# Attention and soft mixture of experts on one core: a load asked for earlier and two small steps of the opening changed in order

## The chip, the cores and the metric

The kernel runs on one core of a Trainium2 chip. The metric is the device time of one execution in microseconds (us), the median of several runs. The core has five engines that work side by side, each through its own queue of instructions in order: TensorE (PE: matrix products and transposes), VectorE (DVE), ScalarE (ACT), GpSimd (POOL), and SyncE (SP), which here issues every transfer (DMA). Engines wait for one another through semaphores. Tiles lie in SBUF; TensorE writes its results to PSUM, of which the kernel uses eight tiles of one bank each.

## The reference

There are 8 batches of 8 heads, with 576 tokens and 64 values a head. The attention has a decay: the logarithm of a gate `f` is summed along the tokens, and the difference of two such sums is added to the score. The result is the input of a soft mixture of 8 experts with 4 slots each.

```python
scores = scale * np.matmul(q, k.transpose(0, 1, 3, 2))
cum = np.cumsum(np.log(np.clip(f, 0.0001, 1.0)), axis=-1)
scores = np.where(causal, -1e9, scores + cum[:, :, :, None] - cum[:, :, None, :])
attn = softmax(scores); x = attn @ v          # heads side by side: 4608 x 512
logits = x @ phi                              # 4608 x 32
slot_input = softmax(logits, axis=0).T @ x    # 32 slots
slot_out = relu(slot_input @ w1) @ w2         # by expert, 4 slots each
out = softmax(logits, axis=1) @ slot_out
```

## The kernel before

**Units.** The 64 heads are worked through in 32 pairs. Pair `g` holds heads `2g` and `2g+1`. Its queries and keys arrive in one load of 128 x 2 x 576 float32 values (`load_qk`, line 165) into one of three buffers, `RAW[g % 3]`: queries in rows 0 to 63, keys in rows 64 to 127. Its values arrive with `load_v` (line 170) into one of two halves of `V`.

**Two passes of products for a head.** The operands are rounded to a short form (fp32r) on ScalarE: `round_k` into `WA`, `round_q` into `YA` (lines 174 to 182), three buffers each. Beside the rounded values, some rows of these tiles carry the summed gates (`load_cum`) and the negative maximum of each query row. What the rounding left off is made on GpSimd (`low_k`, `low_q`, lines 199 to 208) into halves of `WB` and `YB`, two buffers each. The other halves of `WB` and `YB` are copies of the rounded operands, made by the transfers `dup_k` and `dup_q` (lines 190 to 197).

- The first pass, `s1` (line 213), makes scores with queries down the partitions, in four PSUM banks out of a set of three that is used in turn (tag `s`). `tops` (line 228) runs over them on VectorE and leaves the maximum of each query row.
- The maxima are turned by a transpose on TensorE and copied back as a row of `YA`. For pair 0 this is `first_rows` (line 560), in two steps separated by `yield`: five transposes, then two copies on ScalarE. For later pairs it is `mturn` and `mrows` (lines 242 to 259), with a transfer.
- The second pass, `s2` (line 261), makes the scores again with keys down the partitions, in six segments, each a product of the rounded operands (line 274) and one of the rest (line 275), into a ring of three PSUM banks. `expo` (line 278) takes the exponential on ScalarE and frees the bank. `causal` (line 283) sets what lies above the diagonal to zero on GpSimd.
- `s3` (line 301) multiplies with the values, fifty products a head; `norm` (line 316) divides on VectorE; `px` and `xcopy` turn the result for the logits.

**Order.** All order is written out by hand: a call in the Python program appends instructions to the queues of the engines it names, and nothing is reordered later. `warm(n, a)` (line 486) appends `n` products whose result nobody reads, to fill TensorE.

**The opening** (lines 492 to 647) prepares pairs 0 and 1 and the first pass of pair 2. It runs ahead of the main loop, whose pass `g` (line 681) does the second pass, masks, `s3` and `norm` of pair `g` and the first pass of heads `2g+3` and `2g+4`. `first(i, n, busy)` (line 573) appends products `n` of head `i`, then `busy` fillers, then the maxima of these products. `both(i, n)` appends products of the second pass and the exponential. In the opening, the load of pair 3 into `RAW[0]` stands at line 621, behind the transfers of `mrows(1, 0, 1)`, `load_v(1)`, `phis` and `mk`. `RAW[0]` also holds pair 0, whose last readers are `low_k(1)` and `low_q(1)` (lines 553 and 554). The roundings of pair 3 (lines 646 and 647) stand last in the opening, so in ScalarE's queue they come ahead of every exponential of the main loop's first pass, `g = 1`.

The queue of SP around the change holds, in order: `load_qk(2)`, `load_v(0)`, `dup_k(1)`, `dup_q(1)`, `load_cum(2)`, `mrows(1, 0, 1)`, `load_v(1)`, `phis`, `mk`, `load_qk(3)`, `mrows(1, 1, 2)`, `dup_q(2)`, `dup_k(2)`, `load_cum(3)`.

Of the kernel before, what the change touches and what calls it, by code (L numbers as in the profile page):

```python
# [24 lines left out]
WARM = (11, 1)  # L25
# [45 lines left out]
def attn_softmoe(ctx: ExitStack, tc: tile.TileContext, qk, v, f, phi, w1, w2, cst, out):  # L71
# [6 lines left out]
    cs = const.tile([P, 258], F32, name="cs")  # L78
# [69 lines left out]
    def pair(g):  # L148
        return 0 <= g < NG
# [15 lines left out]
    def load_qk(g):  # L165
        if pair(g) and ("r", g) not in st:
            st["r", g] = RAW[g % 3]
            nc.sync.dma_start(RAW[g % 3], qk[g])
# [5 lines left out]
    def round_k(g, *hs):  # L174
        if pair(g):
            for h in hs or range(2):
                nc.scalar.copy(WA[g % 3][0:64, S * h : S * h + S], RAW[g % 3][64:128, h])  # L177

    def round_q(g, *hs):
        if pair(g):  # L180
            for h in hs or range(2):
                nc.scalar.copy(YA[g % 3][0:64, h, 64:640], RAW[g % 3][0:64, h])  # L182
# [7 lines left out]
    def dup_k(g, h0=0, h1=2):  # L190
        if pair(g):
            s = slice(S * h0, S * h1)
            nc.sync.dma_start(WB[g % 2][64:128, s].bitcast(F32), WA[g % 3][0:64, s].bitcast(F32))

    def dup_q(g, h0=0, h1=2):
        if pair(g):
            nc.sync.dma_start(YB[g % 2][0:64, h0:h1].bitcast(F32), YA[g % 3][0:64, h0:h1, 64:640].bitcast(F32))
# [15 lines left out]
    def s1(i, *which):  # L213

        if not head(i):
            return
        g, h = divmod(i, 2)
        ya, wa, m = YA[g % 3], WA[g % 3][:, S * h : S * h + S], TOP[g % 3]
        for n in which:
            bank, o, blk, j0, w = TOPS[n]  # L220
            if o == 0:
                st["top", i % 2, bank] = scratch(False, f"s{i}_{bank}")
            t = st["top", i % 2, bank]
            nc.tensor.matmul(  # L224
                t[:, o : o + w], ya[0:m, h, 128 * blk : 128 * blk + 128], wa[0:m, j0 : j0 + w], start=True, stop=True
            )

    def tops(i, *which):
        if not head(i):
            return  # L230
        g, h = divmod(i, 2)
        for n in which:
            bank, o, blk, j0, w = TOPS[n]
            t = st["top", i % 2, bank]
            m0 = max(448 - (128 * blk + 64) + j0, 0)
            top = MT[g % 3][:, NBLK * h + blk : NBLK * h + blk + 1] if g else m2[h][:, blk, 1:2]
            nc.vector.tensor_tensor_reduce(  # L237
                out=t[:, o : o + w], in0=t[:, o : o + w], in1=mask[:, m0 : m0 + w], scale=1.0, scalar=top if n == 3 else -3.0e38,
                op0=ALU.add, op1=ALU.max, accum_out=top,
            )  # L240
# [245 lines left out]
    def warm(n, a, w=192):  # L486

        for _ in range(n):
            nc.tensor.matmul(ring[0][:, 0:w], a[:, 0:128], a[:, 0:w], start=True, stop=True)
# [83 lines left out]
    def first(i, n, busy=0):  # L573
        s1(i, *GROUPS[n])
        warm(busy, cs)
        tops(i, *GROUPS[n])
# [5 lines left out]
    r0, r1 = first_rows(0), first_rows(1)  # L582
    for n in range(4):
        first(0, n, WARM[1])
    first(1, 0, 2 * WARM[1])
    next(r0)
    warm(3 * WARM[1], cs)
    next(r0)
    round_q(1, 0)
    first(1, 1)  # L590
    first(1, 2)
    both(0, 0)
    first(1, 3)
# [1 line left out]
    both(0, 2)  # L595
    round_k(1, 1)
    round_q(1, 1)
    dup_k(1)
    dup_q(1)
    load_cum(2)  # L600
# [17 lines left out]
    load_v(1)  # L618
    nc.sync.dma_start(phis, phi)
    nc.sync.dma_start(mk, cst[:, 706:714])  # L620
    load_qk(3)
    round_q(2)
    both(1, 2)
    first(3, 1)
# [439 lines left out]
```

## Time and profile before

| | |
|---|---|
| median of 3 runs | 405.67 us (404.69 to 407.14) |
| the profiled execution | 407.26 us |
| its span, first to last instruction | 405.5 us |
| TensorE products busy | 385.3 us (95%) |
| VectorE busy | 281.7 us (69%) |
| ScalarE busy | 259.2 us (64%) |
| GpSimd busy | 257.6 us (64%) |
| mean granted TensorE clock | 0.986 |

A row of the order of instructions gives the start in us from the begin of the span, the length in us, the engine, the line of the kernel, the operation, the tile written and the tiles read with their shapes, and how many instructions are merged in the row (x). In brackets stands how long the engine was idle ahead of it, and what it is inferred to have waited for. Where several semaphores were waited for, the one named is the last that the profile shows; where the engine named had long been done, the real one was another, often a transfer. A row of stretches gives start and end, the length, the busy time of each engine with its count of instructions, the granted clock of TensorE (1.00 is full speed), the busy share of the 16 DMA engines, and GB/s.

### The profile page before, as it was taken

Reading aid. Unit: us, or ns where it says so; the run is one execution under the profiler, and the core shown is the slowest. Engines: PE = TensorE matmul, PEld = TensorE weight load, DVE = VectorE, ACT = ScalarE, POOL = GpSimd, SP = SyncE. Lnnn points to the kernel's source line nnn. Section 1 sums busy time; section 2 is a strip of 40 time slices with the busy share of each in tenths; the row PEclk is TensorE's granted clock in tenths of the full one; section 3 lists DMA queues with packets and bytes.
Section 4 is the critical chain, followed back from the end, with each engine's and each line's share of the span. In section 5 each row is a group of like instructions: output and inputs, shape, how many; then the busy total and the mean of one; then the engine's idle time right before and its main releaser. Section 6 shows DMA issues by size and latency. Waiting matters only on the chain.

```text
span 405.5 us, 15191 instructions
## 1 busy us (share of the span) xinstructions
PE 385.3 (95%) x5871; PEld 339.3 (84%) x5871; DVE 281.7 (69%) x1127; ACT 259.2 (64%) x660; POOL 257.6 (64%) x351
## 2 busy tenths in 40 slices
PE   7888999999999999999999999999999999899990
PEld 6678999999999999998999999999999885345780
DVE  7784787878787977796879787878787533312571
ACT  8847776767786777686767786778685443100561
POOL 4694788777777777787778777877787742120000
PEclk9996999999999999999999999999999999999997
DMA  6773566677867787768767767777765699999698
GB/s 207 183 183 108 150 174 181 204 205 210 254 192 221 207 238 211 203 191 254 200 197 210 221 205 206 205 207 206 203 172 152 227 360 375 381 408 391 239 368 335
DMA packets 35192, 93.72 MB, mean 231 GB/s; under 512 B 4282, under 2 KB 10096, under 8 KB 35120
## 3 DMA queue, kind: packets, MB, share of 16 engines
q1 hardware_dynamic: 35120, 92.75, 74.0%
q8 instruction: 46, 0.75, 0.8%
q14 instruction: 26, 0.21, 0.1%
HBM read 63.93 MB, written 9.73 MB: 182 GB/s over the span
## 4 chain that ended last, share of the span: by engine, by line
PE 81%; DMA 4%; DVE 3%; ACT 3%; issue 1%; POOL 0%; SPq 0%; DVEq 0%; ACTq 0%
PE pv L309 24%; PE ring L274 13%; PE ring L275 11%; PE s L224 11%; PE pv L336 4%; DMA RAW<-in_qk 3%; PE lg L372 2%; PE pv L911 2%; PE ds L453 2%; PE ring L874 2%; PE pv L874 2%; PE more L992 2%; DVE s L237 1%; DMA out<-RAW 1%; PE ring L911 1%; PE ring L992 1%
## 5 line engine op out<-in xcount | busy, mean ns | idle before, releaser
L281 ACT ACTIVATE PTS<-ring 128x320 f32<-128x320 f32 (+2 forms) x256 | 119.7, 513 | 64.3 <-PE ring L275 36.7
L237 DVE CUSTOM_DVE_ANT_0 s<-s,mask 128x320 f32<-128x320 f32 (+4 forms) x320 | 137.7, 449 | 10.4 <-PE s L224 5.9
L274 PE MATMUL ring<-YA,WA 67*128 67x320 f32 (+9 forms) x384 | 123.3, 334 | 2.7 <-ACT PTS L281 1.7
L275 PE MATMUL ring<-YB,WB 128*128 128x320 f32 (+4 forms) x384 | 111.7, 299 | 0.0
L309 PE MATMUL pv<-V,PTS 128*64 128x65 f32 x3200 | 105.0, 224 | 0.6 <-ACT mr L256 0.6
L309 PEld LDWEIGHTS pv<-V,PTS 128*64 128x64 f32 x3200 | 100.3, 138 | 3.2 <-issue 1.2
L224 PE MATMUL s<-WA,YA 66*128 66x288 f32 (+9 forms) x384 | 98.9, 314 | 1.6 <-ACT YA L182 0.8
L203 POOL TENSOR_TENSOR WB<-RAW,WB 64x576 fp32r<-64x576 f32 x64 | 90.3, 1411 | 11.7 <-DMA WB<-WA 4.9
L208 POOL TENSOR_TENSOR YB<-RAW,YA 64x576 fp32r<-64x576 f32 x64 | 89.3, 1413 | 2.4
L274 PEld LDWEIGHTS ring<-YA,WA 67*128 67x128 f32 (+3 forms) x384 | 70.6, 185 | 9.0 <-issue 2.1
L275 PEld LDWEIGHTS ring<-YB,WB 128*128 128x128 f32 (+1 forms) x384 | 70.8, 184 | 0.0
L224 PEld LDWEIGHTS s<-WA,YA 66*128 66x128 f32 (+1 forms) x384 | 63.6, 192 | 7.3 <-ACT YA L182 1.1
L289 POOL TENSOR_SCALAR_AFFINE_SELECT PTS<-PTS 128x384 f32<-128x384 f32 x64 | 33.3, 521 | 32.0 <-ACT PTS L281 27.8
L292 POOL TENSOR_SCALAR_AFFINE_SELECT PTS<-PTS 128x128 f32<-128x128 f32 (+1 forms) x128 | 31.3, 265 | 34.8 <-ACT PTS L281 32.1
L237 DVE DVE_READ_ACCUMULATOR2_ANT MT<- 128x1 f32 x372 | 52.7, 142 | 0.0
L177 ACT CAST WA<-RAW 64x576 fp32r<-64x576 f32 x64 | 40.0, 669 | 14.2 <-DMA RAW<-in_qk 13.2
L336 PE MATMUL pv<-cs,X 128*128 128x128 f32 x155 | 42.9, 278 | 1.0 <-DVE X L329 0.8
L182 ACT CAST YA<-RAW 64x576 fp32r<-64x576 f32 x64 | 40.0, 670 | 0.4
L237 DVE CUSTOM_DVE_ANT_0 s<-s,mask,MT 128x288 f32<-128x288 f32 x62 | 32.6, 526 | 9.8 <-PE s L224 0.9
L324 DVE TENSOR_SCALAR rl<-pv 128x5 f32<-128x5 f32 x64 | 10.5, 164 | 34.7 <-PE pv L309 33.8
L329 DVE TENSOR_TENSOR X<-pv,rl 128x320 f32<-128x320 f32 (+1 forms) x65 | 31.5, 486 | 2.4 <-DMA YA<-mr 0.3
L360 ACT COPY XT<-pv 128x128 f32<-128x128 f32 (+1 forms) x124 | 28.7, 292 | 0.0
(202 smaller groups left out, 355.1 us busy)
## 6 DMA issues: line engine op xcount, KB each, us to landing
w<-in_w SPq DMA_DIRECT2D x46, 512.0 KB
RAW<-in_qk SPq DMA_DIRECT2D x31, 576.0 KB
V<-in_v SPq DMA_DIRECT2D x32, 325.0 KB
WB<-WA SPq DMA_DIRECT2D x31, 288.0 KB
YB<-YA SPq DMA_DIRECT2D x31, 288.0 KB
p<-in_w SPq DMA_DIRECT2D x7, 512.0 KB
out<-RAW SPq DMA_DIRECT2D x5, 512.0 KB
out<-RAW SPq DMA_DIRECT2D x9, 256.0 KB
```

Of the source, the lines that this page charges most:

```text
L177: nc.scalar.copy(WA[g % 3][0:64, S * h : S * h + S], RAW[g % 3][64:128, h])
L182: nc.scalar.copy(YA[g % 3][0:64, h, 64:640], RAW[g % 3][0:64, h])
L203: nc.gpsimd.tensor_tensor(t[0:64], RAW[g % 3][64:128, h], t[64:128].bitcast(F32), op=ALU.subtract)
L208: nc.gpsimd.tensor_tensor(YB[g % 2][64:128, h], RAW[g % 3][0:64, h], YA[g % 3][0:64, h, 64:640].bitcast(F32), op=ALU.subtract)
L224: nc.tensor.matmul(t[:, o : o + w], ya[0:m, h, 128 * blk : 128 * blk + 128], wa[0:m, j0 : j0 + w], start=True, stop=True)
L237: nc.vector.tensor_tensor_reduce(out=t[:, o : o + w], in0=t[:, o : o + w], in1=mask[:, m0 : m0 + w], scale=1.0, scalar=top if n == 3 else ...
L274: nc.tensor.matmul(o, wa[0:m, j0 : j0 + n], ya[0:m, h, 64 + i0 : 64 + i0 + w], start=True, stop=False)
L275: nc.tensor.matmul(o, wb[:, j0 : j0 + n], yb[:, h, i0 : i0 + w], start=False, stop=True)
L281: nc.scalar.activation(PT[i % 2][:, SEG_O[bank] : SEG_O[bank] + at], t[:, 0:at], AF.Exp, scale=0.125)
L289: nc.gpsimd.affine_select(d3, d3, pattern=[[0, 3], [1, 128]], compare_op=ALU.is_ge, fill=0.0, base=0, channel_multiplier=-1)
L309: nc.tensor.matmul(o[64 * u : 64 * u + 64, t, :], PT[i % 2][:, at : at + 64], V[:, g % 2, c, 65 * h : 65 * h + 65], start=(c == 0), stop=( ...
L336: nc.tensor.transpose(pm[:, 0:128], x[:, t, 128 * (p % 2) : 128 * (p % 2) + 128], ident)
```

## The change

Three things are changed, all in the opening. `load_qk(3)` moves up in SP's queue, from behind `mk` to ahead of `dup_k(1)`. The second product group of head 1, `first(1, 1)`, moves from behind `round_q(1, 0)` to ahead of head 0's transposes (the first `next(r0)`). And the fillers around it change in number: two behind the first group of head 1 become one behind each of the first two groups, and three behind the transposes become two, so one filler in all goes. No other instruction is added or taken away.

```diff
     for n in range(4):
         first(0, n, WARM[1])
-    first(1, 0, 2 * WARM[1])
+    first(1, 0, WARM[1])
+    first(1, 1, WARM[1])
     next(r0)
-    warm(3 * WARM[1], cs)
+    warm(2 * WARM[1], cs)
     next(r0)
     round_q(1, 0)
-    first(1, 1)
     first(1, 2)
     both(0, 0)
     first(1, 3)
...
     round_k(1, 1)
     round_q(1, 1)
+    load_qk(3)
     dup_k(1)
     dup_q(1)
     load_cum(2)
...
     load_v(1)
     nc.sync.dma_start(phis, phi)
     nc.sync.dma_start(mk, cst[:, 706:714])
-    load_qk(3)
     round_q(2)
```

## The prediction

> **What bounds the kernel now.** I read the page first, then the busy time of each engine in chosen stretches, then the order of instructions of one engine at a time around the places that the change touches. The page's line of the TensorE clock, in slices of 10.1 us, has one hole in its middle, the fourth slice:
>
> ```profile
> PEclk9996999999999999999999999999999999999997
> ```
>
> The stretches around it (length, then busy us and instructions of each engine, clock, DMA share, GB/s):
>
> ```profile
> 15.57:18.98 3.41, 2.36 (x19) 1.89 (x17) 3.08 (x15) 3.30 (x7) 1.15 (x5) 1.00 0.69 227
> 22.40:25.81 3.41, 3.15 (x73) 2.81 (x69) 2.48 (x13) 1.11 (x4) 3.23 (x5) 1.00 0.68 163
> 29.23:32.64 3.41, 1.74 (x13) 1.51 (x13) 1.64 (x8) 3.39 (x9) 0.91 (x2) 1.00 0.87 283
> 32.64:39.47 6.83, 6.83 (x52) 6.37 (x53) 4.06 (x16) 3.92 (x11) 3.44 (x8) 0.50 0.05 16
> 26.98:41.86 14.88, 12.43 (x145) 11.39 (x143) 8.69 (x35) 9.49 (x21) 8.92 (x12) 0.77 0.53 138
> 41.86:50.73 8.87, 8.87 (x144) 8.48 (x143) 7.25 (x30) 6.82 (x17) 6.90 (x11) 1.00 0.49 142
> ```
>
> The last row is the second pass of the main loop: TensorE is busy for all of its 8.87 us, so a pass is worth what TensorE takes. The first pass, 26.98 to 41.86, does the same work in 14.88 us, 6.01 us more. Of that 3.41 us are the clock: from 32.64 to 39.47 TensorE is busy without a gap at 0.50 (6.83 x 0.5). The rest are gaps:
>
> ```profile
> 23.98 0.38 PE L224 MATMUL s<-WA,YA 66*128 66x288 f32 x1
> 24.61 0.92 PE L309 MATMUL pv<-V,PTS 128*64 128x65 f32 x24 [0.26 <-ACT mr L256]
> ...
> 29.01 0.33 PE L336 MATMUL pv<-cs,X 128*128 128x128 f32 x1 [0.78 <-DVE X L329]
> ...
> 29.83 0.27 PE L336 MATMUL pv<-cs,X 128*128 128x128 f32 x1
> 31.78 0.39 PE L274 MATMUL ring<-YA,WA 67*128 67x256 f32 x1 [1.67 <-ACT PTS L281]
> ```
>
> 0.78 us before 29.01 wait for VectorE's normalisation, 1.67 us before 31.78 for an exponential of ScalarE, which has to free a bank of the ring. ScalarE's order tells why that exponential is late:
>
> ```profile
> 24.30 0.25 ACT L256 CAST mr<-pv 5x128 fp32r<-5x128 f32 x1 [1.05 <-PE pv L247]
> 28.78 1.24 ACT L177 CAST WA<-RAW 64x576 fp32r<-64x576 f32 x2 [4.22 <-DMA RAW<-in_qk]
> 30.04 1.25 ACT L182 CAST YA<-RAW 64x576 fp32r<-64x576 f32 x2
> 31.19 1.17 ACT L281 ACTIVATE PTS<-ring 128x448 f32<-128x448 f32 x3
> ```
>
> The roundings of the fourth pair (round_k(3), round_q(3)) stand ahead of the first pass's exponentials in ScalarE's queue and wait 4.22 us for that pair's load. SP issues the load at 23.56, so it took 5.22 us:
>
> ```profile
> 13.87 0.33 SPq L172 DMA_DIRECT2D V<-in_v  x1
> 17.09 0.48 SPq L193 DMA_DIRECT2D WB<-WA  x1
> ...
> 23.56 0.37 SPq L168 DMA_DIRECT2D RAW<-in_qk  x1
> ```
>
> So the chain is: late load, late roundings, late exponential, TensorE idle, and behind it the slow clock.
>
> **Part one, the load.** load_qk(3) moves in SP's queue from behind phis and mk to ahead of dup_k(1), the row at 17.09, which waits there for ScalarE's rounding. It writes RAW[0], whose last reader is low_q(1), the first row here:
>
> ```profile
> 13.86 1.42 POOL L208 TENSOR_TENSOR YB<-RAW,YA 64x576 fp32r<-64x576 f32 x1
> ...
> 20.38 1.41 POOL L203 TENSOR_TENSOR WB<-RAW,WB 64x576 fp32r<-64x576 f32 x1 [1.57 <-PE ring L275]
> ...
> 23.82 0.49 POOL L292 TENSOR_SCALAR_AFFINE_SELECT PTS<-PTS 128x128 f32<-128x128 f32 x2
> ```
>
> It ends at 15.28, so SP issues the load at about 15.3 in 0.37 us and is free long before 17.09: the issue itself costs nothing. Even at the 5.22 us of the old load it lands by 20.5, before ScalarE is free at 24.55 (24.30 + 0.25). The roundings then run from 24.57 to 27.1 (28.78 to 31.29 is 2.51 us), and the first exponential follows its own product, which stands ahead of the row at 29.01. An exponential takes 0.6 us with its signal (31.19 to 31.78), so the ring is free by 29.6, before TensorE asks at 30.10 (29.83 + 0.27). **The gap of 1.67 us goes: -1.67.**
>
> **The clock.** In the stretch before the drop TensorE was busy for 1.74 of 3.41 us; at 2.36 of 3.41 (15.57 to 18.98) the clock stayed at 1.00. Without the gap the first of these has 1.74 + 1.67 = 3.41 busy. The 0.78 stays, but alone it leaves 2.63 of 3.41. I take the drop to go: **-3.41**. Its bounds are 0 (it comes anyway) and 3.41. What speaks against it is a rule of the Trainium skill, "TensorE: Matmul & The Clock Gate", section "HAM oscillation — how this bites in real kernels": only gaps of TensorE over some 3.4 us bring the half clock. By it a gap of 1.67 us is too short to be the cause. The trace doesn't agree: the longest gap is 1.67 us and 0.50 follows it. Rival A is priced from the rows.
>
> **What the load is put in front of.** Behind it are dup_k(1), dup_q(1) and load_cum(2), on the same DMA engines. What these did:
>
> ```profile
> 14.25:17.50 3.25, 3.16 (x25) 2.86 (x23) 2.85 (x12) 2.73 (x6) 1.93 (x5) 1.00 0.85 283
> 17.50:18.00 0.50, 0.50 (x4) 0.30 (x2) 0.43 (x2) 0.50 (x2) 0.00 (x0) 1.00 0.00 0
> 18.00:21.25 3.25, 2.20 (x15) 1.93 (x15) 2.75 (x13) 3.18 (x9) 1.35 (x3) 1.00 0.92 182
> ```
>
> The third pair's load and load_v(0), 590 kB and 333 kB by their shapes, fill the first stretch; then nothing moves for half a microsecond; then the duplicates go. low_k(2) (20.38) idled 1.57 us for dup_k(1): the row names TensorE, but the operands it reads are the pair's load and that duplicate. At 333 GB/s (283 over the share of 0.85) the first two loads end at about 17.0 and the moved one 1.8 us later, at 18.8, where the duplicates began at 18.0. If the engines take transfers in the order asked, the duplicates come **0.8 us** later. The bounds are 0 (the transfers mix, and the idle half microsecond takes them) and 2.5: a load as slow as the one of 23.56 lands at 20.5. I take 0.8, from the row of the same kind of load at the same place.
>
> GpSimd then works without a pause from low_k(2) to the last mask of causal(1), whose end moves from 24.31 to 25.11. s3(1), at 24.61 in TensorE's queue, reads what it masks, and follows it by 0.05 or so. It starts **0.5 us** later (bounds -0.2 and 2.2), with all of TensorE and the normalisations behind it. load_cum(2) and dup_q(1), late by the same, are asked for later than low_k(2) is; the V load, phis and mk lose a neighbour.
>
> **Part two, the second head's products.** TensorE and ScalarE in the opening, and VectorE's last pass over head 0:
>
> ```profile
> 11.52 0.50 PE L224 MATMUL s<-WA,YA 97*128 97x320 f32 x2 [0.84 <-ACT YA L182]
> 11.86 0.84 PE L489 MATMUL ring<-cs 128*128 128x192 f32 x4
> 12.53 0.71 PE L565 MATMUL ring<-cs,LG 128*2 128x128 f32 x5
> 13.07 1.14 PE L489 MATMUL ring<-cs 128*128 128x192 f32 x6
> 13.92 0.56 PE L224 MATMUL s<-WA,YA 97*128 97x288 f32 x2
> 14.32 0.37 PE L274 MATMUL ring<-YA,WA 98*128 98x448 f32 x1
> ```
>
> ```profile
> 13.16 0.73 ACT L568 CAST YA<-ring 2x512 fp32r<-2x512 f32 x2 [1.00 <-PE ring L565]
> 13.92 0.67 ACT L182 CAST YA<-RAW 64x576 fp32r<-64x576 f32 x1
> 14.93 1.44 ACT L281 ACTIVATE PTS<-ring 128x448 f32<-128x448 f32 x3 [0.34 <-PE ring L275]
> ```
>
> ```profile
> 11.47 0.23 DVE L237 CUSTOM_DVE_ANT_0 s<-s,mask 128x64 f32<-128x64 f32 x1
> ```
>
> A filler product is two instructions. Four stand ahead of the transposes before and after the change (one product's worth moves), and one product of head 1 joins them: the transposes come later by 0.15 to 0.2 us (two such products fill 13.92 to 14.32). Its bank is free: VectorE's passes over head 0 stand ahead of the row at 11.47. The copies of 13.16 to 13.89 then end at about 14.05. Behind the transposes four fillers stand in place of six, 0.14 us each (13.07 to 13.92), and one product in place of two: TensorE comes to the first s2 product at about 13.95 and starts it with the copies, at 14.1 in place of 14.32. That is 0.2 us gained, on TensorE and on ScalarE's exponentials behind. It lies under GpSimd's wait for the duplicates, since s3(1) now follows causal(1): **0.0**. If the duplicates aren't late, it counts, and s3(1) comes 0.2 earlier. VectorE's pass over the moved product fills time in which it had nothing to do.
>
> **The sum.** The profiled execution took 407.26 us (405.5 us of span and 1.76 around it). 407.26 - 1.67 - 3.41 + 0.5 + 0.0 = **402.7 us**. That execution is 1.6 us above the median of the runs, 405.67; half of its loss by the clock would be 1.7 us, so the median run may have had a shorter drop. From there it is 405.67 - 1.7 - 1.67 + 0.5 = 402.8, the same place. That reading of the median is an assumption. Half a per cent of 405.67, about what a measurement of this kernel can tell, is 2.03: faster means under 403.64, slower over 407.70.
>
> **The rivals.** *A, the clock falls anyway*: the gap of 1.67 us was not its cause, or the gaps that are left, 1.0 us before s3(1) (0.26 + 0.5 + the 0.2 that TensorE comes earlier) and 0.78 before 29.01, suffice. Only 1.67 - 0.5 is won. With the whole drop the time is 406.1, with half of it 404.4. For it: nothing in the trace shows where between 1.74 and 2.36 of 3.41 the clock gives way. Against it: the stretch of 22.40 to 25.81 keeps 3.15 - 0.7 = 2.45 busy, more than the 2.36 that kept the clock. That the gap was not the cause is what the rule of the Trainium skill named above says.
>
> *B, the duplicates come so late that the gap only moves* (the other side). If the load takes 5.22 us again, from 15.3 to 20.5, dup_k(1) starts 2.5 us late, causal(1) ends at 26.8 and s3(1) waits 2.2 us. The stretch of 22.40 to 25.81 then has 3.15 - 1.2 = 1.95 busy, under the 2.36 that kept the clock, so it falls there: 407.26 - 1.67 + 2.2 = 407.8, slower. It decides from a lateness of about 0.9 to 1.1 us on (with or without the 0.2 of part two), where that stretch comes under 2.36. For it: 5.22 us was a real load. Against it: that one shared the engines with both duplicates, phis and V.
>
> *C, another wait takes the place.* The fifth pair's load waits for RAW[1], read by low_q(3) until about 28 (after 23.82, two subtractions of 1.4 each and the 0.8), and with 5.22 us lands at 33.3. A first pass of 8.87 + 0.78 us from 27.5 ends at 37.2 and needs its roundings, 2.5 us, some 3 us before that, so there is 1 us in hand. If it or VectorE costs 1 to 2 us of the gain, the time is 403.7 to 404.7: about 404.2.
>
> *D, the duplicates aren't late.* Then s3(1) comes 0.2 earlier in place of 0.5 later: 402.0.
>
> **How the numbers follow.** Forecast 0.55, A 0.17, B 0.08, C 0.12, D 0.08. The predicted time is 402.7; the likeliest case alone holds 401.7 to 403.7, from the bounds of the duplicates' lateness up to 1.5 us and the spread of the runs shown, 404.69 to 407.14. The range goes from 401.3, under D, to 405.7, over C and the half drop of A; the whole drop and B lie outside. Faster: the forecast but for 0.05 of it, D, and 0.02 of C, 0.60. Slower: B and 0.02 of A, 0.10. Same: the rest, 0.30.
>
> **What the profile after would show.** Right: SP issues the load at about 15.3; ScalarE rounds the fourth pair at about 24.5 without waiting for a DMA; no gap of TensorE before the product of the fourth segment; clock 1.00 from 30 to 40, the first pass in 9.5 to 10 us. The step on the duplicates: low_k(2) at about 21.2, s3(1) at about 25.1. Step two: the first exponential at about 14.75 where it was 14.93. Wrong would be the forecast with a clock of 0.50 anywhere between 25 and 40, with low_k(2) past 22, or with a wait of ScalarE for the fifth pair's load.

## The result, and the profile after

| | before | after |
|---|---|---|
| median, in runs beside each other | 407.35 us (403.45 to 410.59, 12 runs) | 404.37 us (401.37 to 411.32, 12 runs) |
| the profiled execution | 407.26 us | 402.23 us |
| its span | 405.5 us | 400.5 us |
| its mean granted clock | 0.986 | 0.992 |

The ratio is 0.9932, with a 95% interval of 0.9903 to 0.9962: the kernel is 0.7% faster. The forecast was 402.7 of 405.67 us, a ratio of 0.9927. That the two ratios agree so well is luck: with more runs before's median is 407.35 and no longer 405.67, and the median after lies 1.7 us above the forecast. An execution more than 1.5% above the fastest of its kernel is left out of every ratio here, which also cuts off the longest drops of the clock (10 of before's 35 executions beside the first four experiments), so a ratio understates an edit that ends these drops, and the medians over all runs stand beside it.

The page's line of the clock no longer has its hole:

```profile
PEclk9999999999999999999999999999999999999996
```

The stretches, with the columns of those of before: two of the clock's own stretches, then the first and the second pass of the main loop.

```profile
15.24:18.65 3.41, 2.33 (x21) 2.02 (x19) 2.98 (x13) 3.20 (x7) 1.23 (x6) 1.00 0.99 349
28.89:32.31 3.42, 2.65 (x21) 2.36 (x20) 3.13 (x15) 1.70 (x6) 3.35 (x4) 1.00 0.97 304
28.04:37.93 9.89, 9.12 (x145) 8.53 (x143) 8.25 (x35) 6.83 (x17) 8.98 (x12) 1.00 0.54 148
37.93:46.80 8.87, 8.87 (x143) 8.47 (x143) 7.25 (x30) 6.88 (x18) 7.62 (x11) 1.00 0.63 174
```

The first pass has shrunk from 14.88 to 9.89 us, 4.99 us less, at a clock of 1.00. That is 1.67 + 3.41 but for 0.09. But it begins at 28.04 where it began at 26.98, 1.06 us later. So the second pass begins 3.93 us earlier (41.86 to 37.93), and this lead goes through the main loop. The last 1.1 us of the 5.0 us of span are not in the opening, and nothing in the change explains them: at the last exponentials, near 325 us, the lead has grown to 4.14 us only, and the rest comes behind the main loop.

The orders of SP, ScalarE and TensorE show the links of the chain one by one. SP asks for the load (the first row) ahead of dup_k(1) (the second):

```profile
15.12 0.33 SPq L168 DMA_DIRECT2D RAW<-in_qk  x1
...
17.00 0.48 SPq L193 DMA_DIRECT2D WB<-WA  x1
```

```profile
14.82 1.46 ACT L281 ACTIVATE PTS<-ring 128x448 f32<-128x448 f32 x3
...
24.21 0.26 ACT L256 CAST mr<-pv 5x128 fp32r<-5x128 f32 x1 [1.04 <-PE pv L247]
24.49 1.24 ACT L177 CAST WA<-RAW 64x576 fp32r<-64x576 f32 x2
25.76 1.25 ACT L182 CAST YA<-RAW 64x576 fp32r<-64x576 f32 x2
28.82 0.87 ACT L281 ACTIVATE PTS<-ring 128x448 f32<-128x448 f32 x2 [1.82 <-PE ring L275]
```

The rounding of the fourth pair has no bracket any more: it follows the row before it at once, at 24.49, where it waited 4.22 us. The exponential now waits for its product and no longer for the roundings. On TensorE:

```profile
18.97 0.47 PE L274 MATMUL ring<-YA,WA 98*128 98x448 f32 x1 [1.41 <-ACT YA L568]
...
24.52 0.68 PE L309 MATMUL pv<-V,PTS 128*64 128x65 f32 x14 [0.26 <-ACT mr L256]
25.94 0.65 PE L309 MATMUL pv<-V,PTS 128*64 128x65 f32 x10 [0.74 <-POOL PTS L292]
...
28.04 0.47 PE L274 MATMUL ring<-YA,WA 67*128 67x448 f32 x1
...
30.06 0.33 PE L336 MATMUL pv<-cs,X 128*128 128x128 f32 x1 [0.77 <-DVE X L329]
...
30.88 0.27 PE L336 MATMUL pv<-cs,X 128*128 128x128 f32 x1
30.91 0.36 PE L274 MATMUL ring<-YA,WA 67*128 67x256 f32 x1
```

The product of the fourth segment follows the row before it without a gap (30.88 to 30.91): the 1.67 us are gone. In their place stand 0.74 us in the middle of s3(1): fourteen of its products run ahead of the masks, the other ten wait for them, and split in two the 24 take 1.33 us (0.68 + 0.65) where they took 0.92 together. The masks are late by what GpSimd waits for the duplicate:

```profile
22.16 1.41 POOL L203 TENSOR_TENSOR WB<-RAW,WB 64x576 fp32r<-64x576 f32 x1 [3.44 <-DMA YB<-YA]
25.59 0.49 POOL L292 TENSOR_SCALAR_AFFINE_SELECT PTS<-PTS 128x128 f32<-128x128 f32 x2
```

low_k(2) starts at 22.16, 1.78 us later than in before (20.38). The forecast said 21.2.

One execution is not the whole of it. The profiled executions without a drop ahead of the last 7 us, in which the clock falls in every trace, have a mean clock of 0.992 to 0.996, and one drop of 3.41 us at 0.50 takes 0.0043 from it. So I count a run with 0.9895 or less as one with a drop; where it lies a run without a trace doesn't tell. A single short drop can leave nearly 0.992, so a run of 0.990 or 0.991 may hold one too, and the counts are lower bounds. Of the 70 runs of before beside the experiments, 67 are such, and the three others have 0.990. Of the 12 of the changed kernel 7 are, with a mean of 405.8 us; the five others have 403.0 and lie at 0.992 or above. (One of the seven has a clock of 0.933 on record, which its time of 405.62 us doesn't bear out.) So the change does not end the drops; it makes them less frequent.

### The profile page after: what moved, and what is told of

Its sections match the earlier page's. It is cut to its first block, busy times and chain, and to the rows that moved or that the text cites. A ratio compares the mean times of both kernels' runs of the same rounds, so it can differ in the third digit from the quotient of the medians.

```text
span 400.5 us, 15188 instructions
## 1 busy us (share of the span) xinstructions
PE 381.8 (95%) x5869; PEld 336.2 (84%) x5869; DVE 281.4 (70%) x1127; ACT 259.2 (65%) x660; POOL 258.0 (64%) x351
## 4 chain that ended last, share of the span: by engine, by line
PE 84%; DMA 3%; DVE 2%; ACT 2%; POOL 1%; issue 1%; SPq 0%; DVEq 0%; ACTq 0%
PE pv L309 24%; PE ring L274 13%; PE ring L275 11%; PE s L224 11%; PE pv L336 4%; PE lg L372 3%; PE more L992 2%; PE pv L911 2%; PE ds L453 2%; PE ring L874 2%; PE pv L874 2%; DMA RAW<-in_qk 2%; DMA YB<-YA 1%; PE ring L992 1%; PE lg L992 1%; PE ring L911 1%
## 5 line engine op out<-in xcount | busy, mean ns | idle before, releaser
L274 PEld LDWEIGHTS ring<-YA,WA 67*128 67x128 f32 (+3 forms) x384 | 69.7, 183 | 7.7 <-issue 2.1
L275 PEld LDWEIGHTS ring<-YB,WB 128*128 128x128 f32 (+1 forms) x384 | 69.9, 182 | 0.0
```

Of the source, the lines that this page charges most:

```text
L274: nc.tensor.matmul(o, wa[0:m, j0 : j0 + n], ya[0:m, h, 64 + i0 : 64 + i0 + w], start=True, stop=False)
L275: nc.tensor.matmul(o, wb[:, j0 : j0 + n], yb[:, h, i0 : i0 + w], start=False, stop=True)
```

## The experiments

All kernels compute the whole result. Where products are added, they are fillers that nobody reads.

**The load alone.**

```diff
+    load_qk(3)
     dup_k(1)
...
-    load_qk(3)
     round_q(2)
```

> Only the load of the fourth pair moves ahead of the second pair's duplicates; the order of head 1's products and the fillers stay as before. Theory (all of the gain is the load's): as the whole change, ratio to before 0.993 within 0.002, the second pass of the main loop beginning at about 37.9 us in place of 41.8, the copy of the maxima and the first exponential where they were before (14.93), low_k(2) at about 22 us. Rival (the moved products bring a part of the gain): ratio 0.996 or above, the second pass beginning at 38.3 or later.

Measured: 404.88 us (401.85 to 408.19, 12 runs), ratio 0.9946 (0.9906 to 0.9985); the clock has fallen in 8 of 12 runs. The profiled execution (405.05 us) has GpSimd's low_k(2) at

```profile
23.76 1.41 POOL L203 TENSOR_TENSOR WB<-RAW,WB 64x576 fp32r<-64x576 f32 x1 [4.92 <-DMA WB<-WA]
```

3.4 us late, and TensorE waits for the masks behind it, followed by a drop of the clock, in the order of its instructions and in two stretches:

```profile
27.52 0.65 PE L309 MATMUL pv<-V,PTS 128*64 128x65 f32 x10 [2.16 <-POOL PTS L292]
```

```profile
25.61:29.02 3.41, 1.50 (x25) 1.30 (x27) 0.52 (x4) 1.53 (x3) 3.25 (x5) 1.00 0.67 132
29.02:32.44 3.42, 3.42 (x30) 3.20 (x27) 3.01 (x15) 0.98 (x2) 3.36 (x4) 0.50 0.55 131
```

This is rival B's mechanism: the gap of the late load has moved to the late duplicate, and the half clock with it. Its price is not B's: this execution is 2.2 us faster than the profiled one of before, where B said slower. It doesn't happen in every execution; five of the others lie below 404.5 us. The first exponential (14.94) is where it was, as expected; the second pass begins at 39.96 and not at 37.9, and that is the wait for the masks with its drop, so it doesn't speak for the moved products.

**The products alone.**

```diff
-    first(1, 0, 2 * WARM[1])
+    first(1, 0, WARM[1])
+    first(1, 1, WARM[1])
     next(r0)
-    warm(3 * WARM[1], cs)
+    warm(2 * WARM[1], cs)
     next(r0)
     round_q(1, 0)
-    first(1, 1)
```

> Only head 1's second product group and the fillers move; the load stays behind mk. Theory: the first exponential comes 0.1 to 0.2 us earlier (14.75 to 14.85), and nothing of it arrives, since ScalarE still waits until about 28.8 us for the load: ratio 1.000 within 0.002, second pass at 41.6 to 41.9. Rival (the products bring a part): ratio 0.998 or below, second pass at 41.4 or earlier.

Measured: 403.85 us (401.93 to 408.83, 12 runs), ratio 0.9942 (0.9901 to 0.9983); the clock has fallen in 10 of 12 runs. The profiled execution (407.54 us) is one of the slower ones and keeps the whole chain, with a drop of 10.24 us behind it, in the orders of ScalarE and TensorE:

```profile
28.57 1.25 ACT L177 CAST WA<-RAW 64x576 fp32r<-64x576 f32 x2 [4.15 <-DMA RAW<-in_qk]
```

```profile
31.57 0.43 PE L274 MATMUL ring<-YA,WA 67*128 67x256 f32 x1 [1.61 <-ACT PTS L281]
```

The first exponential comes at 14.80, as forecast, and nothing of it arrives in this execution. But the median is better than the forecast of no effect, and the trace does not say why. Two pairs of kernels that differ in the products alone don't repeat it: the whole change against the load alone has a mean of 404.6 us (standard error 0.7) against 404.6 (0.5), and with the load behind the duplicates it is 402.5 (0.5) against 402.3 (0.3). What made these 12 runs better stays open.

**The load behind the duplicates.** The change, but with the load after dup_k(1), dup_q(1) and load_cum(2):

```diff
-    load_qk(3)
     dup_k(1)
     dup_q(1)
     load_cum(2)
+    load_qk(3)
```

> The whole change, but the load is asked for behind the second pair's two duplicates and the third pair's sums, still ahead of the maxima's transfer. Theory (the load in front makes the duplicates late and costs the main loop 1 us): low_k(2) back at about 20.3 us in place of 22.16, no wait of TensorE for the masks of head 1, the load there before 24.5, the main loop beginning at about 26.9 in place of 28.04 and its second pass at about 36.8: 1.1 us faster than the change, ratio to before 0.990. Rival (the lateness of the duplicates is covered by something else): the same as the change, ratio 0.993, the main loop at 27.8 or later. A third way: the load lands after 24.5 and ScalarE waits for it again, up to 1 us.

Measured: 402.89 us is the median of all 12 runs, two of which were disturbed (594 and 2027 us); the other ten lie between 400.78 and 404.76, with a median of 402.19. Ratio 0.9905 (0.9865 to 0.9946). The clock has fallen in 5 of these ten. In the profiled execution (400.78 us) the orders of GpSimd, SP and ScalarE show

```profile
20.32 1.42 POOL L203 TENSOR_TENSOR WB<-RAW,WB 64x576 fp32r<-64x576 f32 x1 [1.56 <-PE ring L275]
```

```profile
19.00 1.43 SPq L168 DMA_DIRECT2D RAW<-in_qk  x1
```

```profile
24.68 1.24 ACT L177 CAST WA<-RAW 64x576 fp32r<-64x576 f32 x2
```

low_k(2) starts as in before, and the load, asked for at 19.00 instead of 15.12, is in time all the same, with nothing to spare: in the profile of the kernel with the normalisation first, below, it is asked for at 18.93 and ScalarE waits 0.18 us for it. The first pass begins at 27.08 instead of 28.04. So the lateness of the duplicates comes from the load in front of them, and asking for the load ahead of them buys nothing.

**The gap filled.** Before, with five products of two instructions each in the gap and nothing moved:

```diff
         px(g - 1, 1)
+        if g == 1:
+            idle = scratch(False, "idle")
+            for _ in range(5):
+                nc.tensor.matmul(idle[:, 0:192], cs[:, 0:128], cs[:, 0:192], start=True, stop=True)
         s2(h0, 3)
```

> The kernel before with five more filler products (ten instructions, result read by nobody) in the first pass of the main loop, in the 1.67 us in which TensorE waits for the first exponential. The load stays late. Theory (the half clock comes from the idle time): ScalarE still waits for the load until about 28.8, the first exponential is as late as before, but the clock stays at 1.00 from 25 to 40 us and the second pass begins at about 38.4 in place of 41.8; ratio to before 0.993 to 0.996. Rival (the drop is not caused by this gap, which is shorter than the 3.4 us of the rule of the Trainium skill, page TensorE: Matmul & The Clock Gate): clock 0.50 for 6.8 us after the gap as before, second pass at 41.8, ratio 1.000.

Measured: 404.39 us (403.48 to 406.11, 12 runs) against 406.74 in before (35 runs); the ratio is 0.999 (0.9959 to 1.0021) and misses the forecast of 0.993 to 0.996, while the means of all runs are 404.50 and 406.58. The clock has fallen in 4 of 12 runs, where it was 33 of before's 35. The trace of the profiled execution (403.48 us) keeps the late load and the late exponential; only the fillers are new, in the orders of ScalarE and TensorE and in two stretches:

```profile
28.81 1.24 ACT L177 CAST WA<-RAW 64x576 fp32r<-64x576 f32 x2 [4.22 <-DMA RAW<-in_qk]
```

```profile
29.97 1.79 PE L715 MATMUL idle<-cs 128*128 128x192 f32 x10
31.81 0.38 PE L274 MATMUL ring<-YA,WA 67*128 67x256 f32 x1
```

```profile
28.83:32.24 3.41, 3.15 (x21) 2.85 (x21) 2.06 (x9) 3.39 (x7) 1.19 (x1) 1.00 0.86 252
32.24:39.06 6.82, 6.82 (x129) 6.54 (x128) 4.74 (x20) 5.72 (x15) 5.43 (x9) 1.00 0.28 77
```

The load still lands late, the product of the fourth segment still starts at 31.81 (31.78 in before), and the clock stays at 1.00; the second pass begins at 38.77, where 38.4 was forecast and before has 41.8. This separates the two terms of the forecast: TensorE's idleness brings the clock down, not the late load as such, and useless products hold it up.

**The load between the duplicates.** The change, with the load after dup_k(1) and load_cum(2) and ahead of dup_q(1):

```diff
-    load_qk(3)
     dup_k(1)
-    dup_q(1)
     load_cum(2)
+    load_qk(3)
+    dup_q(1)
```

> The whole change, but the load is asked for behind dup_k(1) and load_cum(2) and ahead of dup_q(1). Theory (only the lateness of dup_k(1), which low_k(2) waits for, costs time; dup_q(1) has slack until the main loop): low_k(2) at about 20.3 us, dup_q(1) 1.5 to 3 us late without anybody waiting, no wait of TensorE for the masks of head 1, the main loop beginning at about 27.0: the same as with the load behind both duplicates, ratio 0.990. Rival (any late duplicate, or the full DMA queue, costs): main loop at 27.6 or later, ratio 0.993.

Measured: 403.60 us (402.11 to 404.39, 6 runs), ratio 0.9901 (0.9864 to 0.9938); the clock has fallen in 3 of 6. Profiled (404.37 us), GpSimd and two stretches:

```profile
20.54 1.41 POOL L203 TENSOR_TENSOR WB<-RAW,WB 64x576 fp32r<-64x576 f32 x1 [1.84 <-PE pv L247]
```

```profile
17.37:20.79 3.42, 2.02 (x13) 1.57 (x12) 2.69 (x13) 3.37 (x8) 0.73 (x3) 1.00 0.75 165
20.79:31.03 10.24, 10.09 (x116) 9.05 (x116) 5.34 (x24) 5.08 (x11) 9.09 (x9) 0.50 0.61 140
```

low_k(2) is in time, and the masks of head 1 end at 24.47, 0.16 us later than in before: of the two duplicates dup_k(1) is the one that makes them late. What a late dup_q(1) would cost TensorE this execution can't show, since here the clock fell at another place, behind the opening's stretch of 17.37 to 20.79, in which head 1's second pass waits for the copies of its maxima; at half the clock the main loop begins at 31.17, and 27.0 was forecast.

**More ahead of the duplicates.** The change, with load_v(1) moved ahead of dup_k(1) too:

```diff
     load_qk(3)
+    load_v(1)
     dup_k(1)
...
-    load_v(1)
     nc.sync.dma_start(phis, phi)
```

> The whole change with one transfer more in front of the duplicates: the second pair's values (333 kB) are asked for right behind the moved load, ahead of dup_k(1). Theory (each transfer in front makes dup_k(1) later, and from there on low_k(2), the masks of head 1 and TensorE; the longer gap lets the clock fall): low_k(2) 0.9 us or more later than in the changed kernel (22.16), so at 23.1 or later, the main loop at 28.9 or later, the clock at 0.50 in more of the runs: 1 to 3 us slower than the change, ratio to before 0.996 to 1.001. Rival (what is late is one slow DMA engine, whatever stands in front): low_k(2) at 22 to 23.8 as in the two kernels with the load in front, ratio 0.993 to 0.995.

Measured: 405.04 us (402.91 to 411.52, 12 runs), ratio 0.9943 (0.9907 to 0.9979); the clock has fallen in 7 of 12. In the profiled execution (406.13 us) low_k(2) starts at 23.62, where the load alone had it at 23.76; twice the bytes in front did not double the lateness. The clock fell at 20.70 already and stayed at 0.50 for 10.24 us, so the wait for the masks can't be read. The lateness of low_k(2) fits both theories. The ratio and the count of drops (7 of 12, as in the changed kernel) are those of the rival, by which more bytes in front cost no more, though the interval reaches into the other range.

**The normalisation first.** The kernel with the load behind the duplicates, and VectorE's maxima of head 4's last group moved behind norm(1):

```diff
     norm(0)
-    first(4, 3)
+    s1(4, *GROUPS[3])
     s3(1, 12, None)
...
         norm(h0 - 1)
+        if g == 1:
+            tops(4, *GROUPS[3])
```

> The load behind the second pair's two duplicates, and on VectorE the normalisation of head 1 ahead of the maxima of head 4's last products, which it had behind it. Theory (the wait of 0.78 us of TensorE at the begin of the main loop is VectorE's order alone): the normalisation of head 1 ends at about 28.1 in place of 29.0, the wait goes to 0.1 or less, the bank that the maxima free is back by 29.1, before TensorE asks for it; the second pass of the main loop at about 36.1 in place of 36.9, ratio to before 0.988. Rival (the bank is late instead): a wait of TensorE for the bank of 0.3 us or more, second pass at 36.5 or later, ratio 0.990.

Measured: 401.99 us (400.35 to 405.0, 6 runs), ratio 0.9881 (0.9831 to 0.9932), and a drop in 2 of 6. The wait of 0.77 us for VectorE is gone; what takes its place in the profiled execution is this, on TensorE:

```profile
29.01 0.50 PE L224 MATMUL s<-WA,YA 66*128 66x320 f32 x2 [0.18 <-DVE MT L237]
```

The second pass begins at 36.43 instead of 36.90 with the load behind; 36.1 was forecast, and 36.5 or later under the rival.

**The load behind the duplicates, alone.** Before, with only the load moved to where the third experiment has it:

```diff
     dup_q(1)
     load_cum(2)
+    load_qk(3)
...
-    load_qk(3)
     round_q(2)
```

> Only the load moves, to behind the second pair's two duplicates and the third pair's sums; head 1's products and the fillers stay as before. Theory (the moved products bring 0.1 to 0.2 us where nothing stands in their way, and what their kernel alone showed more than that is the scatter of the load's landing): mean within 0.5 us of the kernel that has both with the load behind, ratio 0.990 to 0.992. Rival (the products are worth more than 1 us by themselves, as the ratio of 0.994 of the kernel with them alone suggests): ratio 0.993 or above.

Measured: 402.02 us (401.72 to 403.63, 5 runs), ratio 0.9875 (0.9835 to 0.9915), and a drop in none of 5 by the count above (two runs have 0.991, and one of them, 403.63 us, may hold one). One moved line does better in the median than the whole change (404.37) and no worse than the whole change with the load behind (402.19); these are other series, and the interval of its ratio overlaps a little with that of the change (0.9903 to 0.9962). Its wait at the second pass of head 1 stands at before's length:

```profile
19.06 0.47 PE L274 MATMUL ring<-YA,WA 98*128 98x448 f32 x1 [1.06 <-ACT YA L568]
```

**Fillers in that wait.** The kernel with the load behind the duplicates, and the changed kernel, each with five filler products ahead of head 1's second pass:

```diff
+    for _ in range(5):
+        nc.tensor.matmul(pv[0][:, 325:453], cs[:, 0:128], cs[:, 0:128], start=True, stop=True)
     both(1, 0)
```

> The kernel with the load behind the duplicates and head 1's products moved, with five filler products (ten instructions, result read by nobody) in the wait of TensorE before head 1's second pass at 18.9 us. That wait is 1.40 us where the products are moved and 1.06 where they are not. Theory (this longer wait lets the clock fall in about half of the runs, which take 10 us or more at half the clock where it does; the fillers keep it up): the wait gone, no drop of the clock before 380 us, mean clock of 0.990 or above in nearly all runs (5 of 10 without the fillers), ratio to before 0.987 to 0.989, 1 us better in the mean than without the fillers. Rival (the drops have another cause): clock of 0.988 and below in half of the runs again, ratio 0.990.

> The whole change with the same five filler products before head 1's second pass. Theory (two causes of the drops remain in the changed kernel, this wait and the wait for the masks of head 1 at 25 us): fewer runs with a mean clock of 0.988 and below than the change has (6 of 11), the rest of them from the wait at 25 us; ratio to before 0.990 to 0.993. Rival A (only the wait at 25 us counts): clock and ratio as of the change, 0.993. Rival B (only the wait at 18.9 counts): no low clocks left, ratio 0.989.

Measured with the load behind: 402.49 us (401.73 to 403.04, 6 runs), ratio 0.9892 (0.9846 to 0.9937), a drop in none of 6 where it was 5 of 10, and a wait of 0.21 instead of 1.40 us. The gain of 1 us in the mean that was forecast did not come: the mean is 402.5 us with and without the fillers. The runs with a drop are gone, and so are the fastest ones (400.78 to 401.0 us without the fillers, 401.73 the fastest with them). The row of the wait:

```profile
18.93 0.47 PE L274 MATMUL ring<-YA,WA 98*128 98x448 f32 x1 [0.21 <-ACT YA L568]
```

Measured with the load in front: 402.99 us (401.88 to 410.64, 12 runs), ratio 0.9913 (0.9872 to 0.9954), a drop in 4 of 12 where it was 7 of 12. In the profiled execution (401.88 us) GpSimd's row is

```profile
21.21 1.40 POOL L203 TENSOR_TENSOR WB<-RAW,WB 64x576 fp32r<-64x576 f32 x1 [2.54 <-DMA WB<-WA]
```

which is the lateness of 0.8 us that the prediction gave for the change, and no wait for masks is left; its first pass begins at 27.07. With the load in front the drop stays in a third of the runs although this wait is filled; with the load behind it is gone. The ratio flatters, because three of the four runs with a drop (408.8 to 410.6 us) lie over its limit: the mean of all 12 is 404.7 us, as in the changed kernel (404.6). The numbers of runs are small, and they leave open how much of the rest is the masks' wait.

**The best put together.** The load behind the duplicates alone, with the normalisation first, and then the same with four filler products ahead of head 1's second pass:

```diff
     load_cum(2)
+    load_qk(3)
...
+    for _ in range(4):
+        nc.tensor.matmul(pv[0][:, 325:453], cs[:, 0:128], cs[:, 0:128], start=True, stop=True)
     both(1, 0)
...
-    first(4, 3)
+    s1(4, *GROUPS[3])
...
         norm(h0 - 1)
+        if g == 1:
+            tops(4, *GROUPS[3])
```

> The load behind the duplicates, the normalisation of head 1 ahead of the maxima of head 4's last products, head 1's products and the fillers as before. Theory: no wait for the load, no wait for the masks, a wait of 0.2 us in place of 0.78 at the begin of the main loop, second pass at about 36.4, few drops of the clock since the wait at 18.9 us is 1.06 us: ratio to before 0.986 to 0.987, the fastest so far. Rival (the gain of 0.5 us by the normalisation is lost to something else): as the load behind alone, 0.9875 to 0.990.

> As the kernel before it, with four filler products in the wait of TensorE before head 1's second pass. Theory: the clock never falls before 380 us, in any run; ratio 0.985 to 0.987, with the smallest spread of the runs. Rival (the fillers delay head 1's second pass or the clock falls elsewhere): ratio 0.988 or above.

Measured without the fillers: 402.35 us (401.5 to 404.65, 6 runs), ratio 0.9893 (0.9840 to 0.9946), in the range of its rival and not the 0.986 to 0.987 that was forecast. A drop in 1 of 6 (a second run, of 0.990 and 404.44 us, may hold one), in the profiled execution:

```profile
17.57:20.98 3.41, 2.35 (x14) 1.90 (x14) 2.91 (x13) 3.36 (x9) 1.09 (x3) 1.00 0.81 160
20.98:24.39 3.41, 3.41 (x41) 3.19 (x41) 2.13 (x12) 2.25 (x6) 3.19 (x6) 0.50 0.93 270
```

With the fillers: 401.88 us (401.26 to 402.42, 6 runs), ratio 0.9878 (0.9833 to 0.9924), just above the 0.985 to 0.987 that was forecast, and no drop, as forecast. The fillers delay head 1's second pass by 0.23 us (19.29 instead of 19.06). It has the smallest median and the smallest spread of all, 1.2 us from lowest to highest, against 6.7 us in the 17 runs of before beside it. It is faster than before, and its median is below that of the changed kernel, which was measured in another series; against the single moved line (402.02) the medians differ by less than these runs can tell.

## Why the prediction was right, and where it was not

**The load (-1.67): right.** Issued at 15.12 (forecast 15.3), roundings at 24.49 (24.5) without a wait, no gap ahead of the fourth segment's product, the first pass in 9.89 us (9.5 to 10). That SP's queue and not the transfer's own speed made it late is shown by the load behind the duplicates, which is in time as well.

**The clock (-3.41): right in the profiled execution, too sure over the runs.** That idleness of TensorE in the first pass brought the drop is shown by the filled gap: the load as late as ever, the clock at 1.00, and a drop in 4 of 12 runs instead of 33 of 35. The rule of the Trainium skill named in the prediction ("TensorE: Matmul & The Clock Gate", section "HAM oscillation — how this bites in real kernels") doesn't hold in these traces: the longest single gap ahead of a drop in the opening or the first pass was between 1.05 and 2.16 us. What failed is the step "2.36 of 3.41 kept the clock", read as a mark: at 2.35 busy the clock fell in one trace and held in another, and at 2.25 it held. The prediction also counted the busy time in the stretches of before's profiled execution as if they lay there in every run. They don't: the same wait of 1.40 us ahead of head 1's second pass lost no clock with the load behind, where a stretch began at 15.35 and another at 18.76, and lost it with the load between, where one began at 17.37. And the step "the drop goes" looked for gaps between 25 and 40 us alone. The wait ahead of head 1's second pass, at 18.97, was in the prediction's own stretches and was not followed. So rival A, "the clock falls anyway", which was priced at 404.4 to 406.1 us, is true of 7 of 12 runs (mean 405.8), and that is most of the 1.7 us between the forecast of 402.7 and the median of 404.37, since the five runs without a drop have 403.0. That the gaps behind it are the masks' wait and head 1's wait is argued from the kernels beside it, where the traces caught drops there (the load alone, the load between); the one profile of the changed kernel holds no drop.

**The duplicates (+0.5): right in kind, too small.** The step that was mis-sized is the lateness of 0.8 us from "the engines take transfers in the order asked". It was 1.8 us in the profiled execution of the changed kernel, 0.8, 3.4 and 3.2 in three others with the load in front (low_k(2) at 21.21, 23.76, 23.62), and at most 0.2 in those with the load behind. "low_k(2) past 22" was among the prediction's own signs of being wrong, and with 22.16 it came. The main loop began 1.06 us later, not 0.5. The bounds of the lateness, 0 and 2.5, hold the changed kernel's 1.8, but two of the four profiles with the load in front go beyond them. That s3(1) as a whole waits was wrong too: fourteen of its products need no mask, so only the last ten are late.

**Part two (0.0): right in size, for an incomplete reason.** The first exponential came at 14.82, 0.11 us earlier than 14.93 and not 0.2. What the part does besides was missed: TensorE runs out of products 0.46 us earlier (17.56 instead of 18.02), but the copies of head 1's maxima stand behind an exponential in ScalarE's queue and come only 0.10 earlier (18.18 instead of 18.28), so the wait ahead of its second pass grew from 1.05 to 1.41 us. That this makes the clock fall more often is argued from counts over the kernels with the load behind the duplicates: a drop in 7 of 16 runs with the products moved (5 of 10, and 2 of 6 with the normalisation first), in 1 of 11 without (none of 5 and 1 of 6), and in none of 12 with the wait filled. The comparison with the filled wait is the stronger one; that moving the products brings the drops is less sure, since five of the eleven runs have a clock of 0.990 or 0.991.

**The sum and the median.** 402.7 was forecast against the profiled execution's 407.26, and 402.23 came. That is closer than the terms deserve: the opening brought 3.93 us and not 4.58, which would make 403.3, and 1.1 us were won elsewhere without a cause in the change. The assumption that the median run of before had had a shorter drop fell: in larger numbers before's median is 406.7 to 408.3, and 67 of 70 runs show a drop. So the second way to the forecast, from the median (402.8), had no ground, and its agreement with the first was chance.

**The rivals.** B's mechanism was seen (the load alone), C not: in the changed kernel ScalarE's roundings of the fifth pair, at 35.47, wait for nothing (in the two profiles of 402.11 and 401.62 us with the normalisation first they wait about 0.5 us for that load). D's condition holds in the kernels with the load behind, whose medians of 401.9 to 402.5 us lie at what D was priced at (402.0).

## What to carry to other kernels

When a late transfer has to be asked for earlier, put it behind the small transfers that somebody is already waiting for, and not ahead of them: the load could be asked for 3.9 us later and was still in time, if only just; the duplicates had nothing in hand. Where a clock drop follows a gap, look at every gap around it and not at the longest one alone, and try fillers in it first, since they tell whether the idleness or the lateness costs the time. Judge such a kernel by many runs and count the ones with a drop: one profiled execution shows one of several outcomes.

## What the runs showed of the hardware

The clock's drops start on a grid of 3.41 us, at another place of the kernel in each execution: in before the half clock begins at 32.64 and, at the end of the kernel, at 401.28, which is 108 steps of 3.413 us, and the other five traces with an early drop give whole steps too. The Trainium skill speaks of a free-running window of that length ("TensorE: Matmul & The Clock Gate", section "What's actually happening"), and the traces agree. In the opening and the first pass, drops came behind stretches of the grid with 1.29, 1.50, 1.74, 2.01, 2.02 and 2.35 us busy of 3.41; the clock held behind 2.25, 2.33, 2.35, 2.36 and 2.65, two of which are these rows, of the kernel with the load behind and of that load alone:

```profile
15.35:18.76 3.41, 2.25 (x20) 1.95 (x18) 2.98 (x13) 3.19 (x8) 2.62 (x7) 1.00 0.74 249
```

```profile
17.92:21.33 3.41, 2.35 (x17) 2.00 (x16) 2.92 (x14) 3.34 (x9) 1.44 (x3) 1.00 0.94 184
```

So busy time as the profile counts it gives no sharp mark. Near the end of the kernel it gives none at all: these two stretches of the grid in before have 2.05 and 1.87 us busy, and the clock stays at 1.00 behind both.

```profile
350.08:353.49 3.41, 2.05 (x21) 0.84 (x17) 0.84 (x4) 0.44 (x2) 1.56 (x3) 1.00 1.03 412
353.49:356.91 3.42, 3.42 (x49) 1.32 (x41) 0.00 (x0) 0.42 (x2) 0.31 (x1) 1.00 1.02 410
394.45:397.87 3.42, 1.87 (x9) 1.17 (x7) 2.08 (x3) 1.47 (x3) 0.00 (x0) 1.00 1.05 395
397.87:401.28 3.41, 0.00 (x0) 0.00 (x0) 0.00 (x0) 0.00 (x0) 0.00 (x0) 1.00 1.05 405
```

What the clock goes by besides stays open. Once fallen, it stayed at 0.50 for one stretch in two traces (3.41 us), for two in one (6.83) and for three in three (10.24), though TensorE was busy nearly all the time. The Trainium skill gives the full clock back after at least one busy window (same page and section); one was enough in two of these six traces, and in the four others it was not. And a copy from SBUF to SBUF that stands behind a load is late by another amount each time (low_k(2) from 21.21 to 23.76); what decides it stays open.
